# Retention and a SwiGLU layer on one core: units of 512 tokens, and an output product of 49 block products

## The chip, the cores and the metric

The kernel runs on one core of one Trainium2 chip. A core has TensorE (PE in the profile; its weight loads are listed apart as PEld), VectorE (DVE), ScalarE (ACT), GpSimd (POOL) and SyncE (SP), which issues most transfers. They work on an on-chip memory of 128 partitions (SBUF); TensorE writes its products to PSUM, eight banks of 512 float32 a partition. The metric is the time of one execution on the device, in microseconds.

## The reference

Retention over 8 batches of 8 heads (sequence 576, head size 64), then an RMS norm and a gated feed-forward layer on the 4608 tokens of 512 features. All matrix data is float32 but for the three weight matrices of the layer, which the kernel receives as float64 words and rounds itself.

```python
scores = scale * q @ k.T                      # per batch and head, 576 x 576
D[i, j] = gamma_h ** (i - j) if i >= j else 0 # gamma_h = 1 - 2**(-5 - h)
x = (scores * D) @ v                          # -> (4608, 512)
xn = x / sqrt(mean(x * x) + 1e-6) * rms_g
g, val = xn @ w_gate, xn @ w_val              # 512 -> 1536, twice
out = (g * sigmoid(g) * val) @ w_out          # 1536 -> 512
```

## The kernel before

A job is a pair of heads of one batch; `slot(j)` does the scores of job j in chunks of 64 rows, with a running state (`sums`), and finishes job j - 1. The feed-forward part runs in 12 units of U = 384 tokens. Units 0 and 1 multiply plainly while the weights are being rounded and combined. From unit 2 on, all products use a scheme that replaces 8 products of 2x2 blocks with 7, at the price of sums and differences of blocks: `up` for the two input products, `across` for the output product.

```python
U = 384; HU = U // 2; NH = 6                 # tokens of a unit, of a half, blocks of 128 of half of 1536
w_out = const.tile([P, NF, DM], F32)          # later four slots for blocks of w_out read back from DRAM
w_up = [const.tile([P, 7 * 2, NH * P], F32) for n in ("w_gate", "w_val")]   # all 7 blocks, resident

def up(u, m, g):                              # 3 g x 2 m of them per unit
    def product(blk, ps, start):
        for i in range(2):
            for c in range(2):
                nc.tensor.matmul(ps[:, i * HU : i * HU + HU], lhsT=w_up[m][:, 2 * blk + c, cut],   # L611
                                 rhs=t_of[u][blk][:, c], ...)
    # ... seven products, each followed by adds of the kind of add/result on VectorE (L618, L628):
    product(A22, w, False)
    result(f + NH, 0, "c21", u2, w)

def differences(u):                           # two block differences of h, 1152 elements each (L726)
    for o, a, b in ((t1, b12, b11), (b12, b22, b12)):
        nc.vector.tensor_tensor(out=o, in0=a, in1=b, op=ALU.subtract)

def across(u):                                # seven products of 12 matmuls, weights stationary
    def product(rhs, ps, start, ...):
        for i in range(2):
            for c in range(NH):
                nc.tensor.matmul(ps[:, i * HU : i * HU + HU], lhsT=a[:, c, i * P : i * P + P],     # L742
                                 rhs=rhs[:, c], ...)
    # ... x, z, w, y, x, z, w; block updates of h between them (L755), results turned by a
    #     32x32 transpose on VectorE (L764) and stored in rows of 32 elements

def root_1(u):                                # the norm of the next unit: mean of squares by a product
    nc.tensor.matmul(s, lhsT=ones, rhs=y, start=True, stop=True)                                   # L529
    # ... then two root steps on ScalarE and VectorE
# main loop, unit u: six up stages with up to four slots between them; then
rest = across(u); next(rest)                  # differences
behind(u, 5)                                  # a slot, then norm_0(u + 1): squares and three sums
for i, _ in enumerate(rest):                  # one step per product
    if i == 2: behind(u, 6)                   # root_1(u + 1)
    elif i == 3: root_2(u + 1)
    elif i == 4: behind(u, 7)                 # norm_2(u + 1): scaling of x, its differences
```

The rounding of the weights (`exponent`, `mantissa`, `join`) runs on VectorE and ScalarE during the first two units; GpSimd combines the blocks of w_gate and w_val (`combine`, L949) after that.

Of the kernel before, what the change touches and what calls it, by code (L numbers as in the profile page):

```python
# [14 lines left out]
P = 128  # L15
L = P // 2
# [25 lines left out]
def kernel(  # L42
# [21 lines left out]
    U = 384  # L64
# [3 lines left out]
    NH = NF // 2  # L68
    NG = NH // 2
    EPS = 1e-6  # L70
    K0, K1 = 2.38924456, 0.703952253
    assert (D, DM, NHP * P) == (64, H * D, DM) and S % SQ == 0 and NTOK % U == 0
    assert NC * L == S and NC == 2 * NFULL + 1 and TAIL == L == D and NHP == 4 and NH % 2 == 0
    assert (2 * S) % U == 0 and B % 2 == 0 and S == 3 * HU

# [4 lines left out]
    ffn = ctx.enter_context(tc.tile_pool(name="ffn", bufs=1))  # L80
    tmp = ctx.enter_context(tc.tile_pool(name="tmp", bufs=6))
    outs = ctx.enter_context(tc.tile_pool(name="outs", bufs=3))
# [22 lines left out]
    top = cell("top", 255.0 * 2.0**23)  # L105
    causal = const.tile([P, L], F32, name="causal")
# [8 lines left out]
    guess = cell("guess", 0x5F1FFFF9 + 2.0**22 * np.log2(DM))  # L115
    w_out = const.tile([P, NF, DM], F32, name="w_out")
# [3 lines left out]

    A11, A12, S1, A22, S2, S3, S4 = range(7)
    A21 = S1

    w_up = [const.tile([P, 7 * 2, NH * P], F32, name=n) for n in ("w_gate", "w_val")]

    CUT = HU // L
    parts = [(0, 0, NC), (1, 0, CUT), (1, CUT, NC)] + [(b, 0, NC) for b in range(2, B)]
    jobs = [(b, hp, c0, c1) for b, c0, c1 in parts for hp in range(NHP)]
    LATER_JOBS = 3 * NHP
    st = [{} for _ in jobs]
    x_of, t_of, h_of, first_places = {}, {}, {}, {}

    def tiles_of(j):

        return jobs[j][2] // 2, min((jobs[j][3] + 1) // 2, NFULL)

    def load_qk(j):
        b, hp, c0, _ = jobs[j]
        for nm, src in (("q", q), ("k", k)):

            t = raw.tile([P, S // SQ, SQ], F32, tag=nm + "raw", name=f"{nm}raw_{j}")  # L150
            for e in range(2):
                rows = src[b, 2 * hp + e, c0 * L :]
                rows = rows.rearrange("(t b) (i a) -> i b t a", b=SQ, a=SQ)
                for i in range(D // SQ):
                    r = e * D + i * SQ
                    nc.sync.dma_start(out=t[r : r + SQ, c0 * L // SQ :], in_=rows[i])
            st[j][nm + "raw"] = t

    def load_first(j, tails):

        b, hp, *_ = jobs[j]
        d = st[j]
        tiles = tiles_of(j)[1]
        room = h_of[0].rearrange("p f t -> p (f t)")
        part = room[:, j * 4 * P : j * 4 * P + tiles * P]
        d["q"] = part.rearrange("p (e t d) -> p e t d", e=2, d=D)
        nc.sync.dma_start(
            out=part.rearrange("p (e t) -> p e t", e=2),  # L170
            in_=q[b, 2 * hp : 2 * hp + 2, : tiles * P].rearrange("e (p t) d -> p e (t d)", p=P),
        )
        for nm, src in (("k", k), ("v", v)):
            t = first_places[nm][j][:, : tiles * P].rearrange("p (c e d) -> p c e d", e=2, d=D)
            d[nm] = t
            for e in range(2):
                nc.sync.dma_start(
                    out=t[:, :, e],
                    in_=src[b, 2 * hp + e, : tiles * P].rearrange("(c p) d -> p c d", p=P),
                )  # L180
            for n in (0, 1) if nm == "k" else (2,):
                load_tails(b, n, tails)

    def find_places():

        n = NFULL * 2 * D
        kv = {
            nm: [raw.tile([P, n], F32, tag=nm, name=f"first_{nm}_{i}", bufs=bufs) for i in range(bufs)]
            for nm, bufs in (("k", 4), ("v", 3))
        }  # L190
        other = raw.tile([P, S], F32, tag="qraw", name="first_k_7")[:, :n]
        sums = [ffn.tile([P, 3 * 2 * HU], F32, tag=t, name=f"first_{t}") for t in ("sums", "t1")]
        room = h_of[0].rearrange("p f t -> p (f t)")[:, 2 * NHP * 4 * P :]
        more = w_up[1][:, 8:].rearrange("p b f -> p (b f)")[:, 6 * DM :]
        return {
            "k": kv["k"] + kv["v"] + [other],
            "v": [t[:, i * n : i * n + n] for t in sums for i in range(2)]
            + [more[:, i * n : i * n + n] for i in range(3)] + [room],
        }

    def load_tails(b, n, heads):


        if heads:
            room = w_up[1][:, 8:].rearrange("p b f -> p (b f)")
            nm, src = (("qt", q), ("kt", k), ("vt", v))[n]
            t = room[:TAIL, (3 * b + n) * DM : (3 * b + n + 1) * DM]
            t = t.rearrange("p (h d) -> p h d", d=D)
# [7 lines left out]
    def load_kv(j):  # L216

        b, hp, *_ = jobs[j]
        i0, _ = tiles_of(j)
        for nm, src, bufs in (("k", k, 4), ("v", v, 3)):  # L220
            t = raw.tile([P, NFULL, 2, D], F32, tag=nm, name=f"{nm}_{j}", bufs=bufs)
            for e in range(2):
                rows = src[b, 2 * hp + e, i0 * P : NFULL * P]
                nc.sync.dma_start(
                    out=t[:, i0:, e], in_=rows.rearrange("(c p) d -> p c d", p=P)
                )
# [18 lines left out]
    def turn(j, waits=(0, 0)):  # L245


        d = st[j]
        n = tiles_of(j)[1]
        for nm in "qk":  # L250
            if nm == "k":
                warm_up(waits[0], 4 * P)
# [15 lines left out]
        if jobs[j][3] < NC:  # L268
            return
# [923 lines left out]
```

## Time and profile before

The time is 1136.91 us, the median of two runs (1136.47 and 1137.35); the profiled execution spans 1134.0 us.

| what | value |
|---|---|
| TensorE busy | 1118.2 us, 99% |
| VectorE, ScalarE, GpSimd busy | 732.3, 258.9, 39.5 us |
| moved | 126.73 MB, mean 112 GB/s |
| granted clock of TensorE, mean | 0.997 |
| window 0 to 45 us | TensorE busy 37.24 us, VectorE 30.98, 219 GB/s |
| window 242 to 331 us (unit 2) | TensorE busy 88.46 us of 89, VectorE 62.44, 120 GB/s |

How to read it: the busy table gives each engine's busy time and number of instructions; matmuls are pipelined, so a busy TensorE says only that products are in flight. The line of 40 digits gives the busy share by slice of 28 us. A group's line has the line number, engine, operation, output and inputs, their shape, the count, then the busy time of the group and the mean ns of one, then the idle time before it and what ended it. A timeline line has the start in us, how long the run of equal instructions took, the engine and the instruction. The chain of work that ended last is listed in order of time as start, duration, engine, tile and count.

### The profile page before, as it was taken

The numbers are of one execution on the slowest core, as the hardware profiler recorded it, in microseconds if no ns is written. First come the engines' busy times: TensorE is split into PE (matmuls) and PEld (weight loads), VectorE is DVE, ScalarE is ACT, GpSimd is POOL, SyncE is SP. The second block draws the span as 40 slices with busy tenths as digits, with TensorE's granted clock in tenths as the row PEclk, the third lists the DMA queues.
The fourth block names the chain that finished last, engine by engine and source line by source line (L and its number), as shares of the span: only waits on it lengthen the run. The fifth ranks groups of instructions, "written<-read, shape, count | busy, mean of one in ns | idle before, by whom it ended". The sixth has DMA issues, their size and how long they took to land.

```text
span 1134.0 us, 24783 instructions
## 1 busy us (share of the span) xinstructions
PE 1118.2 (99%) x10456; PEld 1042.7 (92%) x10456; DVE 732.3 (65%) x1452; ACT 258.9 (23%) x508; POOL 39.5 (3%) x68
## 2 busy tenths in 40 slices
PE   8899999999999999999999999999999999999998
PEld 6655567999999999999999999999999999999998
DVE  5888878556775784485677585465676666446352
ACT  5565551011212211211211121121120210120110
POOL 0100000560000000000000000000000000000000
PEclk9899999999999999999999999999999999999999
DMA  9743587336264474062552555215436503303304
GB/s 226 221 149 112 141 179 223 57 64 166 55 143 107 103 165 134 1 131 79 123 127 45 139 147 100 112 54 102 137 69 135 154 6 99 126 1 101 123 1 112
DMA packets 307040, 126.73 MB, mean 112 GB/s; under 512 B 284528, under 2 KB 289904, under 8 KB 306928
## 3 DMA queue, kind: packets, MB, share of 16 engines
q1 hardware_dynamic: 302640, 123.66, 43.1%
q8 instruction: 82, 1.34, 0.5%
q10 hardware_dynamic: 4288, 1.48, 0.5%
q14 instruction: 30, 0.25, 0.1%
HBM read 110.14 MB, written 14.94 MB: 110 GB/s over the span
## 4 chain that ended last, share of the span: by engine, by line
PE 93%; DVE 2%; DMA 2%; ACT 2%; issue 1%; SPq 0%; POOL 0%; POOLq 0%; DVEq 0%; ACTq 0%
PE x L611 14%; PE w L611 14%; PE z L611 14%; PE xo L742 8%; PE wo L742 8%; PE zo L742 8%; PE up L668 8%; PE y L611 7%; PE yo L742 4%; PE av L406 2%; PE s L323 1%; PE av L428 1%; PE s L345 1%; ACT w_gate L906 1%; PE ms L529 1%
## 5 line engine op out<-in xcount | busy, mean ns | idle before, releaser
L635 ACT COPY m<-x 128x384 f32<-128x384 f32 x60 | 28.8, 479 | 338.7 <-PE x L611 338.7
L742 PE MATMUL xo<-h,w_out 128*128 128x192 f32 x528 | 90.3, 328 | 0.0
L611 PE MATMUL x<-x,w_gate 128*128 128x192 f32 x480 | 88.8, 328 | 0.5 <-issue 0.5
L611 PE MATMUL w<-sums,w_val 128*128 128x192 f32 x480 | 88.6, 328 | 0.3
L611 PE MATMUL x<-x,w_val 128*128 128x192 f32 x480 | 88.7, 328 | 0.0
L611 PE MATMUL w<-sums,w_gate 128*128 128x192 f32 x480 | 87.9, 326 | 0.0
L611 PE MATMUL z<-x,w_gate 128*128 128x192 f32 x480 | 87.8, 326 | 0.0
L611 PE MATMUL z<-x,w_val 128*128 128x192 f32 x480 | 87.8, 326 | 0.0
L742 PEld LDWEIGHTS xo<-h,w_out 128*128 128x128 f32 x528 | 85.9, 190 | 0.6
L742 PE MATMUL wo<-h,w_out 128*128 128x192 f32 x504 | 85.6, 326 | 0.4 <-DVE c_last L790 0.4
L618 DVE TENSOR_TENSOR u<-m,y 128x384 f32<-128x384 f32 x60 | 33.1, 552 | 79.1 <-PE y L611 79.1
L742 PEld LDWEIGHTS wo<-h,w_out 128*128 128x128 f32 x504 | 82.4, 190 | 0.7 <-DVE c_last L790 0.7
L611 PEld LDWEIGHTS w<-sums,w_val 128*128 128x128 f32 x480 | 79.2, 190 | 2.7 <-DVE c L618 2.7
L611 PEld LDWEIGHTS x<-x,w_gate 128*128 128x128 f32 x480 | 79.2, 190 | 1.3 <-issue 0.8
L611 PEld LDWEIGHTS x<-x,w_val 128*128 128x128 f32 x480 | 79.1, 190 | 0.6
L611 PEld LDWEIGHTS z<-x,w_val 128*128 128x128 f32 x480 | 79.6, 190 | 0.0
L611 PEld LDWEIGHTS z<-x,w_gate 128*128 128x128 f32 x480 | 79.6, 190 | 0.0
L611 PEld LDWEIGHTS w<-sums,w_gate 128*128 128x128 f32 x480 | 79.5, 190 | 0.1
L618 DVE TENSOR_TENSOR h<-u,w 128x384 f32<-128x384 f32 x60 | 33.0, 550 | 69.8 <-PE w L611 69.8
L630 ACT ACTIVATE h<-h 128x384 f32<-128x384 f32 x90 | 47.0, 523 | 88.6 <-DVE h L618 88.6
L668 PE MATMUL up<-x,w_gate 128*128 128x384 f32 x192 | 63.8, 489 | 0.7 <-DVE x L580 0.7
L668 PE MATMUL up<-x,w_val 128*128 128x384 f32 x192 | 63.5, 488 | 0.2 <-DVE h L674 0.2
(189 smaller groups left out, 1779.5 us busy)
## 6 DMA issues: line engine op xcount, KB each, us to landing
w_out<-w_blocks SPq DMA_DIRECT2D x70, 768.0 KB, 4.9
out_dram<-o SPq DMA_DIRECT2D x364, 24.0 KB, 1.6
qraw<-in_q_dram SPq DMA_DIRECT2D x96, 72.0 KB, 2.7
kraw<-in_k_dram SPq DMA_DIRECT2D x96, 72.0 KB, 2.7
k<-in_k_dram SPq DMA_DIRECT2D x48, 128.0 KB, 2.8
v<-in_v_dram SPq DMA_DIRECT2D x48, 128.0 KB, 2.9
w_out<-in_moe_w_gate_dram SPq DMA_DIRECT2D x5, 1024.0 KB, 8.3
w_out<-in_moe_w_val_dram SPq DMA_DIRECT2D x3, 1024.0 KB, 5.2
```

Of the source, the lines that this page charges most:

```text
L323: nc.tensor.matmul(s[side(odd), e, i * L : i * L + L], lhsT=d["kT"][side(e), c * L : c * L + L], rhs=d["qT"][side(e), c * L : c * L + L], ...
L345: nc.tensor.matmul(o[side(e)], lhsT=d["k"][side(odd), i, e], rhs=d["v"][side(odd), i, e], start=True, stop=True,)
L406: mm = nc.tensor.matmul(av[odd][column(j, odd, e), i * L : i * L + L], lhsT=d["v"][side(odd), i, e] if c < NC - 1 else d["vt"][:, e], rhs= ...
L428: mm = nc.tensor.matmul(av[odd][column(j, odd, e), i * L : i * L + L], lhsT=d["sum"][c - 1][side(e)], rhs=d["qT"][side(e), c * L : c * L + L],
L529: nc.tensor.matmul(s, lhsT=ones, rhs=y, start=True, stop=True)
L611: nc.tensor.matmul(ps[:, i * HU : i * HU + HU], lhsT=w_up[m][:, 2 * blk + c, cut], rhs=t_of[u][blk][:, c], start=(start and i == c == 0), ...
L618: nc.vector.tensor_tensor(out=o, in0=a, in1=pairs_of(ps), op=ALU.add)
L630: nc.scalar.activation(out=o, in_=c, func=AF.Silu)
L635: nc.scalar.copy(out=s1, in_=pairs_of(x_))
L668: nc.tensor.matmul(ps[:, :U], lhsT=w_up[m][:, 4 * half + c, i * P : i * P + P], rhs=x_of[u][:, c], start=(c == 0), stop=(c == NHP - 1),)
L742: nc.tensor.matmul(ps[:, i * HU : i * HU + HU], lhsT=a[:, c, i * P : i * P + P], rhs=rhs[:, c], start=(start and i == c == 0), stop=False, ...
L906: nc.scalar.activation(func=AF.Relu, **acts.pop(0)[1])
```

## The change

Units become 512 tokens, 9 instead of 12. The output product splits each of its seven block products once more into seven (49 products of 128 tokens x 384 rows x 128 features), with the tokens' `h` blocks stationary and the weights moving, so that its result comes out with tokens on partitions and is stored in rows of 128 elements without a transpose. The inner sums of `h` run on GpSimd, as do the final block sums of a unit and the joining and combining of the weights. All weight blocks, of w_gate and w_val as well as w_out, are written to DRAM once and stream back from unit 2 on through one ring in SBUF. Batch 1 is no longer split into two sets of jobs, so there are 32 jobs instead of 36.

```diff
-    U = 384
+    U = 512
+    NK = NH // 2
...
-    w_out = const.tile([P, NF, DM], F32, name="w_out")
-    w_up = [const.tile([P, 7 * 2, NH * P], F32, name=n) for n in ("w_gate", "w_val")]
+    RING = 17920
+    ring = const.tile([P, RING], F32, name="ring")
...
+    UP, OUT = 7 * 2 * 2 * P, 7 * NK * P       # 1.84 and 1.38 MB over 128 partitions
+    def refill(most=len(pieces)):             # called whenever a piece has been used
+            nc.sync.dma_start(out=ring[:, a:z], in_=src)
...
     def across(u):
+        def inner_sums(n):                    # 128x384 each
+            for o, a, b, op in (
+                (i1, x12, x11, ALU.subtract), (i3, x22, x12, ALU.subtract),
+                (i2, i3, x11, ALU.add), (i4, x21, i2, ALU.subtract),
+            ):
+                nc.gpsimd.tensor_tensor(out=o, in0=a, in1=b, op=op)
+        def product(n, nm, w, late):
+            for s, lhs in (
+                ((S1, i1), (S3, i3), (S2, i2), (A22, i4)) if late
+                else ((A11, x[:, :NK, :P]), (A12, x[:, NK:, :P]), (S4, x[:, NK:, P:]))
+            ):
+                ps = vector[nm][s // 4][:, s % 4 * P : s % 4 * P + P]
+                for c in range(NK):
+                    nc.tensor.matmul(ps, lhsT=lhs[:, c], rhs=w[:, s, c], ...)      # L702
...
+        inner_sums(0)
+        inner_sums(1)
+        yield
+        for n, nm in enumerate("xzwyxzw"):    # x, y, z, w: two PSUM banks each, eight in all
+            product(n, nm, w, False)
+            yield
+            product(n, nm, w, True)
+            ...                               # block updates of h and t1, 1536 elements each, on VectorE;
+            ...                               # adds of PSUM to the sums of the unit (896 elements)
+            if n + 2 < 7:
+                inner_sums(n + 2)
+            yield
+        if not last:
+            combine()                         # seven sums of 128x4x128 on GpSimd; on VectorE in the last unit
...
     for u in range(2, NU):
...
             rest = across(u)
+            if u + 1 < NU:
+                norm_0(u + 1)
             for i, _ in enumerate(rest):
-                if i == 2:
-                    behind(u, 6)
+                if i == 0:
+                    root_1(u + 1)
+                elif i == 4:
+                    root_2(u + 1)
+                elif i == 8:
+                    norm_2(u + 1)
...
+    def join(i):                              # half a chunk of weights: 512 elements
+        nc.gpsimd.tensor_tensor(out=o, in0=x, in1=e, op=ALU.mult)
+    def combine_blocks(t, o21):               # four sums of 512; for w_out four more of 7x128
+            nc.gpsimd.tensor_tensor(out=t[o], in0=t[x], in1=t[y], op=op)
...
+        for u, k in (                         # plain up stages of units 0 and 1, four steps each
+            (0, 0), (0, 1), (1, 0), (1, 1), (0, 2), (1, 2), (0, 3), (1, 3), (0, 4), (0, 5), (1, 4),
+            (1, 5),
+        ):
+            weights_to(READY[k])              # READY = (4, 8, 12, 20, 28, 32) of 36 halves
```

The two sets of w_gate and w_val that lie in SBUF at a time in the plain stage are reused: the halves of set k + 2 are joined only after both units have used set k. In the plain stage `across(0)` and `across(1)` follow each other directly.

## The prediction

> **What bounds the kernel now.** I read the page's busy table and its 40 slices first, then the chain that ended last in order of time, then the groups by shape, and last the timeline and the single-line views around the operations that the change adds.
>
> ```profile
> PE 1118.2 (99%) x10456; PEld 1042.7 (92%) x10456; DVE 732.3 (65%) x1452; ACT 258.9 (23%) x508; POOL 39.5 (3%) x68
> PE   8899999999999999999999999999999999999998
> DVE  5888878556775784485677585465676666446352
> PE 93%; DVE 2%; DMA 2%; ACT 2%; issue 1%; SPq 0%; POOL 0%; POOLq 0%; DVEq 0%; ACTq 0%
> ```
>
> TensorE is busy in every slice and is 93% of the chain; only the first 2 slices have slack. GpSimd does nothing after slice 9. So time can be won only by giving TensorE fewer or cheaper instructions, and lost by making it wait. Its price list comes from the chain (start, us, instructions):
>
> ```profile
> 61.84 67.35 PE up L668 x208
> 404.25 3.90 PE zo L742 x24
> ```
>
> A float32 product is two instructions, each with its own weight load. 67.35/208 = 324 ns for 384 moving columns and 3.90/24 = 162.5 ns for 192: 0.84 ns a column and about 1 ns more. By that, 256 columns cost 216 ns, 512 cost 431, 128 cost 109. Loads are hidden at 192 columns. At 128 columns a load of 128 columns may not be; the only place with loads closer together is the mean of squares, whose moving operand has one column (TensorE, then its loads):
>
> ```profile
> 39.86 0.83 PE L515 MATMUL ms<-mean_w,sq 128*128 128x1 f32 x6 [1.00 <-DVE sq L503]
> 39.86 0.74 PEld L515 LDWEIGHTS ms<-mean_w,sq 128*128 128x128 f32 x6 [1.24 <-DVE sq L503]
> ```
>
> Six loads take 0.74 us with the last one's 0.19 us to its end: (0.74 - 0.19)/5 = 110 ns from load to load. So 128 x 128 x 128 should run at about 111 ns an instruction, set as much by the load as by the product.
>
> GpSimd's price for a tensor_tensor, from the view of one line (min/median/max ns), and one VectorE operation beside it:
>
> ```profile
> L949 POOL TENSOR_TENSOR w_val<-w_val x12: 1267/1272/2262, 211.6 to 227.2; 128x512 f32<-128x512 f32 x12
> L949 POOL TENSOR_TENSOR w_gate<-w_gate x12: 1265/1273/2262, 228.4 to 244.0; 128x512 f32<-128x512 f32 x12
> L755 DVE TENSOR_TENSOR h<-h x22: 1315/1350/1755, 219.0 to 1121.7; 128x1152 f32<-128x1152 f32 x22
> ```
>
> 1.27 us for 512 elements, 1.35 us from one to the next (16.2 us for 12 in the groups). The two outliers of 2262 ns are a wait of 0.99 us each. One of them covers 219 us, where L755, with both inputs in SBUF, took 1755 ns instead of 1350: each waited for the other. VectorE operations with one input in PSUM, which ran beside GpSimd in the same stretch, kept their usual time.
>
> Last, the end of an up stage today:
>
> ```profile
> 396.30 1.57 PE L611 MATMUL w<-sums,w_val 128*128 128x192 f32 x8
> 397.91 0.55 DVE L618 TENSOR_TENSOR c<-u,w 128x384 f32<-128x384 f32 x1
> 400.08 4.17 PE L742 MATMUL xo<-h,w_out 128*128 128x192 f32 x24
> 407.91 0.56 DVE L499 SCALAR_TENSOR_TENSOR sq<-sq,sq 128x384 f32<-128x384 f32 x1
> 411.88 0.81 PE L529 MATMUL ms<-sq,ones 128*128 128x384 f32 x2
> ```
>
> The last square sum (L499) is ready at 408.5, 10 us after the last up product, but the product that needs it (L529) stands behind three output products and doesn't wait.
>
> **What the Trainium skill says.** "TensorE: Matmul & The Clock Gate", section "LDWEIGHTS (loading the stationary operand)": the load's time follows its columns over 1.2 GHz, an estimate of 107 ns for 128; the trace's 110 agrees. "GPSIMD Engine Reference", section "3.1 Elementwise — side-by-side cycle accounting": about 2.6 cycles an element for two inputs, an estimate of 1.1 us for 512 at the 1.2 GHz of its table of specifications; the trace has 1.27. "Advanced Engine Details and Errata", section "GPSIMD Details": GpSimd shares a read and a write interface with VectorE and conflicts with VectorE instructions with two SBUF inputs; the 2262 and 1755 ns agree. The first page's section on the HAM clock gate says that an idle stretch of some 3.4 us halves TensorE's clock; the trace before has no such gap after its start, so nothing here shows it.
>
> **The change, part by part: TensorE's own work.** Before: output 12 units x 168 x 162.5 ns = 328 us; up 10 x 336 x 162.5 = 546; plain up 2 x 192 x 324 = 124; together 998. After: output 9 units x 49 blocks x 3 x 2 = 294 instructions x 111 ns = 32.6 us each, 294 together; up 7 x 336 x 216 ns = 72.6 each, 508; plain up 2 x 192 x 431 = 166; together 968. **30 us are won**, all of it in the output product; up and plain up together neither gain nor lose.
>
> Rest of TensorE's path, without new waits. The first feed-forward product starts at 48 us before; five full attention slots instead of eight (four of them short) stand ahead of it, but the whole norm of unit 0 follows them unhidden: 45 us. Between feed-forward products the timeline before shows 2.35 us for a later attention job; 20 of these are 47 us. Three early and four late jobs in the plain stage with their turns: 20 us. Seven norm products of 512 columns: 6 us. Tail (seven block sums on VectorE, stores): 4 us. 968 + 45 + 47 + 20 + 6 + 4 = **1090 us**, if nothing new waits.
>
> **New waits.** (a) *The norm product at the head of the output stage.* The changed program puts the 512-column product of L464, for the next unit, straight after the last up product and ahead of the first output product, because the output stage needs all eight banks afterwards. It needs the sum of four squares, and in VectorE's order that stands behind c21 (add, multiply), two differences and three gathers. VectorE takes 0.55 us for 384 elements and 1.35 for 1152, so about 0.69 for 512: 0.25 + 7 x 0.72 = 5.3 us after the last up product. All but the first have two SBUF inputs, and GpSimd is at its h sums then; each turn it takes costs one of its operations, 1.0 us (512 to 384 elements by the ratio, 0.95, and the gap): with two or three turns 7 to 8 us. TensorE stands for that time in units 2 to 7: 6 x 7 = **42 us**.
>
> (b) *The sums of unit 0 ahead of the h sums of unit 1.* They are seven GpSimd operations of 512 elements, 9.4 us, and come only after the last add of unit 0 (1.4 us); then four h sums, 4.2 us. The late half of unit 1's first product could start after 2 us and starts after 15: **13 us**, once.
>
> (c) *GpSimd's pace in the output stage.* Four h sums are 4.2 us for each product of 42 x 111 ns = 4.7 us: it keeps up, with 0.5 us to spare. But two-input work of VectorE in the same stage is two block updates of 1536 (1.75 each), three gathers, three root operations and eight of the norm (0.69 each), 13 us a unit. If all of it pushed GpSimd back, the six rounds of h sums after the first would need 25 + 13 = 38 us against 30 until the last is needed. Part of it falls into (a) and into GpSimd's idle time; I take 2 to 3 us for each of six units: **15 us**.
>
> (d) *The plain stage.* GpSimd now joins 36 half chunks (1.35 each), combines six sets (5.4 each) and three slices of w_out (about 14.6 each, the 7x128 sums at 2.3): 125 us. 103 of them lie between step 12 and the end of the stage, a stretch of some 130 us; between steps 12 and 24 it is 36 of 41 us, and VectorE's two-input mantissa work (two of 0.64 us a half) pushes against it. Without the conflict it fits; with all of it, 12 halves x 1.3 us = 16 us make the stage late by 10, and later sets by as much again. I take **15 us**.
>
> Sum: 1090 + 42 + 13 + 15 + 15 = **1175 us**.
>
> **Rivals.** *The gain arrives.* If GpSimd and VectorE hardly meet and (a) is as short as VectorE's own 5.3 us, (a) 32 and (b) 13 remain: 1135, within 2%. For a time under 1114 the wait of (a) must not exist; the program's order speaks against that. *GpSimd becomes the bound.* If the conflict is a strict taking of turns, (c) is 6 to 8 us a unit, 45, (d) is 40, and (a) 50: 1238. The two outliers of 0.99 us speak for turns; but they are two, and most of GpSimd's 24 operations met no such VectorE work. *Transfers bind.* A main unit now moves 11 MB of up and 9.6 MB of output blocks besides 4 to 5 MB of attention: 25 MB in some 120 us, 210 GB/s, against 118 to 120 before; in the output stage 1.38 MB each 4.7 us, 290 GB/s. The first slices reached 226 GB/s with small packets, and the ring holds some five pieces ahead; I expect no wait from this, but should it be one, 3 us a piece over 63 pieces would be far over 1240. *The load isn't hidden* beside a product of its own length: if load and product don't overlap fully at 128 columns and an instruction takes 130 ns, the output stage costs 9 x 294 x 19 ns = 50 us more, though GpSimd's lateness would hide some of it.
>
> **Range and chances.** 1175 us; 1125 (only (a) at its shortest and (b), with a somewhat lower base) to 1225 (turns taken nearly strictly). Under 1114: 0.08. Within 2% (1114 to 1160): 0.27. Slower by over 2%: 0.65.
>
> **What would show it.** Output instructions at 111 ns inside a run of 18 or 24; a gap of 5 to 9 us on TensorE ahead of each L464 product of units 3 to 8, released by the VectorE gather (L429); one of about 13 us early in unit 1's output stage, released by GpSimd (L688); GpSimd operations of 384 elements near 1.0 us with outliers of 1.5 to 2; late halves of some output products released by GpSimd. I'd be wrong if the gap at L464 is under 3 us, if output instructions take over 120 ns, or if releases by DMA of the ring head the list of TensorE's waits.

## The result, and the profile after

The changed kernel takes **1336.5 us** (median of 1335.33 and 1337.71) against 1136.9 before: a ratio of 1.175, with a 95% interval of 1.172 to 1.179. The prediction said slower, but 1175 us in a range that ended at 1225. 161 us more than predicted are to be explained.

The page of the changed kernel: first TensorE's busy time, then three of its lines of 40 slices (33 us each) with the granted clock, then the chain's shares.

```profile
PE 1140.5 (85%) x10086; PEld 937.8 (70%) x10086; DVE 790.6 (59%) x1328; ACT 297.5 (22%) x581; POOL 507.3 (38%) x400
PE   6488967377476999799979997998899799979997
POOL 0312363555167810470066007401730272056026
PEclk7788988689688999899989998999899999989999
DVE 1%; issue 0%; DVEq 0%
```

Before, TensorE had 9s from the third slice on. Now there are two kinds of holes: the first 13 slices are ragged throughout, and from then on one slice in four is a 7 or 8, once for each unit. In both the granted clock (PEclk, in tenths of full speed) dips below 9; before, it did so in the second slice alone. The chain reaches back only 7 us here, to the last sums, so it can't tell where the rest went; the list of TensorE's waits can (total us, times, longest):

```profile
PE up L637 <- POOL ring L871: 51.4, 8, 17.4
PE ms L464 <- DVE sq L429: 42.6, 6, 7.1
PE s L280 <- DVE kT L252: 18.0, 3, 17.6
...
PE ms L445 <- DVE sq L433: 12.5, 1, 12.5
PE s_out L702 <- POOL vi L688: 11.6, 1, 11.6
```

L637 is the plain up product of units 0 and 1, and L871 the join of a half chunk of weights. The second and fifth lines are the waits that steps (a) and (b) named; the first is step (d)'s, over three times as long as I took all of (d) to be.

The end of an up stage, the same place as the last view of before:

```profile
548.44 0.69 DVE L585 TENSOR_TENSOR c<-u,w 128x512 f32<-128x512 f32 x1 [0.31 <-PE w L578]
...
551.10 2.88 DVE L433 TENSOR_TENSOR sq<-sq,sq 128x512 f32<-128x512 f32 x2
...
554.09 1.29 DVE L429 SCALAR_TENSOR_TENSOR sq<-sq,sq 128x512 f32<-128x512 f32 x1
...
555.52 2.04 PE L464 MATMUL ms<-sq,ones 128*128 128x512 f32 x2 [7.12 <-DVE sq L429]
...
557.36 2.64 PE L702 MATMUL s_out<-ring,h 128*128 128x128 f32 x18
```

TensorE has nothing from 548.4 to 555.5. Three gathers take 4.2 us because GpSimd is at its h sums; three in the plain stage, with GpSimd at none, took 0.69 each, 2.1. After the wait two instructions of L464 take 2.04 us and the 18 of L702 2.64 (1.10 and 2.17 in e6 below, without the wait): the record of the clock is at half from 551.5 to 558.3, so L464 and the first of L702 run at half clock. Further into the stage an output instruction comes every 111.5 ns, as worked out.

GpSimd's h sums (min/median/max ns), answering the GpSimd lines of before:

```profile
L688 POOL TENSOR_TENSOR vi<-h x80: 992/998/2595, 339.5 to 1317.1; 128x384 f32<-128x384 f32 x80
L688 POOL TENSOR_TENSOR vi<-t x36: 997/1449/2516, 371.2 to 1321.2; 128x384 f32<-128x384 f32 x36
```

1.0 us undisturbed, with a median of 1.45 for the sums of `t`, which at this place fall beside VectorE's products, differences and gathers.

Now the plain stage, which holds most of the loss. Lines of the timeline from four engines, in order of time (SPq is SyncE's queue: when a transfer was issued):

```profile
176.20 15.57 POOL L880 TENSOR_TENSOR vi<-vi 128x512 f32<-128x512 f32 x8
185.32 2.37 DVE L857 SCALAR_TENSOR_TENSOR ring<-ring 128x512 f32<-128x512 uint32 x1
191.80 8.47 SPq L891 DMA_DIRECT2D w_out_blocks<-vi  x7
193.07 8.83 PE L637 MATMUL up<-x,ring 128*128 128x512 f32 x16 [12.09 <-POOL ring L871]
200.37 1.48 SPq L821 DMA_DIRECT2D sums<-in_moe_w_val_dram  x1
207.04 0.43 DVE L834 TENSOR_SCALAR sums<-sums 128x512 uint32<-128x512 uint32 x1 [19.35 <-DMA sums<-in_moe_w_val_dram]
210.88 2.08 PE L637 MATMUL up<-x,ring 128*128 128x512 f32 x2 [8.97 <-POOL ring L871]
```

Read it downward. GpSimd makes the eight block sums of a w_out slice for 15.6 us; the join that TensorE needs stands behind them in its order (12.09 us). The seven stores of that slice can't go before 191.8 and take 8.5 us to issue, and the load of the next half chunk stands behind them in SyncE's order, until 200.4. VectorE, which would round it, has nothing for 19.35 us, and TensorE stands again (8.97). No engine is busy throughout: in the 296 us from 72 to 368 TensorE is busy 216, VectorE 165, ScalarE 109, GpSimd 118.

### The profile page after: what moved, and what is told of

The parts are those of the page before. It is cut to its first block, busy times and chain, and to the rows that moved or that the text cites. A ratio compares the mean times of both kernels' runs of the same rounds, so it can differ in the third digit from the quotient of the medians.

```text
span 1335.9 us, 24285 instructions
## 1 busy us (share of the span) xinstructions
PE 1140.5 (85%) x10086; PEld 937.8 (70%) x10086; DVE 790.6 (59%) x1328; ACT 297.5 (22%) x581; POOL 507.3 (38%) x400
## 5 line engine op out<-in xcount | busy, mean ns | idle before, releaser
L688 POOL TENSOR_TENSOR vi<-h 128x384 f32<-128x384 f32 x80 | 95.6, 1213 | 512.6 <-DVE h L595 460.6
L637 PE MATMUL up<-x,ring 128*128 128x512 f32 x384 | 186.3, 643 | 56.0 <-POOL ring L871 51.4
L637 PEld LDWEIGHTS up<-x,ring 128*128 128x128 f32 x384 | 76.9, 206 | 159.9 <-issue 88.8
L578 PE MATMUL x<-x,ring 128*128 128x256 f32 x672 | 161.4, 383 | 0.0
L578 PE MATMUL z<-x,ring 128*128 128x256 f32 x672 | 158.8, 379 | 0.0
L578 PE MATMUL w<-sums,ring 128*128 128x256 f32 x672 | 158.7, 379 | 0.0
L578 PEld LDWEIGHTS z<-x,ring 128*128 128x128 f32 x672 | 127.7, 190 | 17.4
L578 PEld LDWEIGHTS w<-sums,ring 128*128 128x128 f32 x672 | 127.7, 190 | 17.4
L578 PEld LDWEIGHTS x<-x,ring 128*128 128x128 f32 x672 | 125.1, 190 | 17.4
L578 PE MATMUL y<-sums,ring 128*128 128x256 f32 x336 | 79.4, 379 | 2.2 <-DVE sum L329 2.2
L702 PE MATMUL s_out<-ring,vi 128*128 128x128 f32 x540 | 69.0, 282 | 11.6 <-POOL vi L688 11.6
L702 PEld LDWEIGHTS s_out<-ring,vi 128*128 128x128 f32 x540 | 65.7, 198 | 12.1 <-POOL vi L688 12.0
L702 PEld LDWEIGHTS s_out<-ring,h 128*128 128x128 f32 x384 | 54.7, 224 | 22.0 <-DVE vi L720 8.3
L702 PE MATMUL s_out<-ring,h 128*128 128x128 f32 x384 | 56.4, 309 | 13.3 <-DVE vi L720 6.8
```

The source lines that it names most:

```text
L578: nc.tensor.matmul(ps[:, i * HU : i * HU + HU], lhsT=w[:, blk, c, i * P : i * P + P], rhs=t_of[u][blk][:, c], start=(start and i == c == 0 ...
L637: nc.tensor.matmul(ps, lhsT=w[:, blk, c % 2, i * P : i * P + P], rhs=x_of[u][:, c], start=(c == 0), stop=(c == NHP - 1),)
L688: nc.gpsimd.tensor_tensor(out=o, in0=a, in1=b, op=op)
L702: nc.tensor.matmul(ps, lhsT=lhs[:, c], rhs=w[:, s, c], start=((nm, s // 4) not in first), stop=False, skip_group_check=True,)
```

## Experiments

Each changes the changed kernel unless it says otherwise. "Stage" is the time from the first plain up product to the first output product, "units 2 to 8" from the first product of `up` to the last product (trace). The times of e10 to e12 are medians of four executions, the others of e1 to e14 are single ones; executions of one kernel side by side differed by up to 4.2 us. The kernel before took 1134.4 to 1138.9 us beside them.

For the plain stage I had three theories. A: SyncE's order, stores that wait ahead of loads and fetches. B: GpSimd and VectorE hinder each other, so that their work takes longer than its sum. C, formed after e1 to e4: pieces are made just in time, and rounding stands still where a join may not go yet. For units 2 to 8 the theory was step (a), the late norm product, and its rival GpSimd's pace.

| run | time, us | first up product at | stage | units 2 to 8 |
|---|---|---|---|---|
| changed kernel | 1336.5 | 71.8 | 303.2 | 866.8 |
| e1_stores_held | 1301.4 | 72.1 | 262.9 | 872.3 |
| e2_norm_later | 1303.8 | 72.1 | 302.0 | 834.2 |
| e3_all_held | 1312.9 | 69.5 | 282.9 | 866.2 |
| e4_joins_on_vector | 1309.1 | 70.6 | 271.1 | 873.1 |
| e5_rounds_ahead | 1305.9 | 71.9 | 270.8 | 867.4 |
| e6_norm_early | 1289.3 | 73.2 | 302.1 | 819.2 |
| e7_start | 1335.8 | 65.9 | 312.9 | 863.0 |
| e8_kept_busy | 1325.4 | 72.2 | 302.3 | 855.6 |
| e9_stores_gpsimd | 1312.5 | 72.1 | 278.9 | 866.8 |
| e10_combined | 1261.6 | 68.2 | 278.8 | 818.6 |
| e11_sets_first | 1249.7 | 68.1 | 269.6 | 817.5 |
| e12_sums_on_vector | 1242.1 | 65.9 | 259.0 | 818.9 |
| e13_no_rounding (leaves out work) | 1224.0 | 51.9 | 210.3 | 867.4 |
| e14_no_block_sums (leaves out work) | 1273.5 | 69.1 | 241.8 | 867.4 |

**e1: stores held back.** The stores of finished blocks are issued three half chunks later, behind the loads.

```diff
-            nc.sync.dma_start(out=w_out_d[o][:, :, k], in_=slices[:, o])
+            held.append((n_joined, lambda o=o: nc.sync.dma_start(...)))   # the same for w_up_d
...
             load_half(i + 4, nc.sync)
+            send(i - 3)
```

> The changed kernel, but the stores of finished weight blocks (L885, L891) are issued three half chunks later, so that the loads of the next halves and of q and k no longer stand behind them in SyncE's order. Theory A (SyncE's order: stores that wait for GpSimd's sums hold up the next loads): the three waits of VectorE for a load in the plain stage (19.4, 16.6, 17.3 us) go, and about 45 us of the 1336.5 with some of TensorE's half-clock time: 1280 to 1295. Theory B (GpSimd and VectorE hinder each other at the shared interface): the loads were no limit, under 15 us: 1322 to 1335.

1301.4, between the two ranges. The waits of up products for joins fell from 51.4 to 25.6 us and the one of 17.6 us for kT went: SyncE's order was a cause. But the last slice's stores now stood behind the attention's fetches, and the first output product waited 19.1 us for its blocks: part of the gain was handed back at the next door.

**e2: norm product later.** In units 2 to 7 `root_1` stands behind the first output product instead of ahead of it.

```diff
-                if i == 0:
+                if i == 2:
                     root_1(u + 1)
```

> The changed kernel, but the norm product of the next unit stands after the first output product instead of ahead of it. If the product waits for VectorE alone, the six gaps of 7.5 us and the half-clock time after each go: 6 x (7.5 + 1 to 2) = 50 to 57 us, 1280 to 1287. If GpSimd sets the pace of the output stage (part (c) of the prediction), the time comes back there as waits for h sums: 1300 to 1336.

1303.8, all of it in units 2 to 8. The number is in the rival's range, but not for its reason: no new wait for h sums is in the list. The wait for the gathers fell from 7.1 to 2.4 us a unit (the gap that I had counted, which holds the norm product too, from 9.3 to 4.3 to 4.6): they are still late for the new place. Five of these six short waits are followed by a record of 3.4 us at half clock, so it doesn't take 7 us of idleness.

**e3: block sums held too.** The sums and stores of a finished block stand four half chunks later.

```diff
-            (finish_set if kind == "up" else finish_slice)(k)
+            held.append((i, lambda: finish(k)))                           # sent four halves later
```

> The changed kernel, but both the block sums on GpSimd and their stores are issued four half chunks later, after the joins of the next set. Theory A and GpSimd's order together: TensorE's waits for joins (51 us for L871, 18 us for kT) nearly go, with the half clock after them: 1255 to 1275, 15 to 30 us under the run that holds the stores alone. If only SyncE's order counts: the same as that run. Theory B: 1322 to 1335, the conflicts being the same.

1312.9, in none of the three ranges and worse than e1, with waits for joins of 36.8 us, the longest 19.1, and 18.7 us again ahead of the first output product. A later place in the order moved the 15 us of a slice's sums ahead of another join.

**e4: joins and block sums on VectorE.**

```diff
-        nc.gpsimd.tensor_tensor(out=o, in0=x, in1=e, op=ALU.mult)         # join
+        nc.vector.tensor_tensor(out=o, in0=x, in1=e, op=ALU.mult)
-            nc.gpsimd.tensor_tensor(out=t[o], in0=t[x], in1=t[y], op=op)  # combine_blocks
+            nc.vector.tensor_tensor(out=t[o], in0=t[x], in1=t[y], op=op)
```

> The changed kernel, but joins and block sums of the weights run on VectorE instead of GpSimd, in the same order. Theory B: the two engines no longer meet in the plain stage, VectorE's weight operations fall back to 0.43 and 0.69 us, which saves some 42 us there against 63 us of added work, and the waits for GpSimd go: 1270 to 1300. Theory A: the stores still stand ahead of the loads, waiting now for VectorE: the loads stay late, 1320 to 1360.

1309.1, above B's range and below A's. What GpSimd had cost VectorE is in the groups. The changed kernel, 72 to 370 us (busy us, mean ns):

```profile
L850 DVE SCALAR_TENSOR_TENSOR ring<-ring 128x512 uint32<-128x512 uint32 x15 | 22.5, 1501 | 1.1 <-ACT ring L828 0.9
L853 DVE TENSOR_SCALAR ring<-ring 128x512 uint32<-128x512 uint32 x15 | 15.8, 1050 | 0.5
```

The same groups of e4, 72 to 335 us, and the slices' sums there:

```profile
L880 DVE TENSOR_TENSOR vi<-vi 128x512 f32<-128x512 f32 (+1 forms) x24 | 21.4, 891 | 0.7
L850 DVE SCALAR_TENSOR_TENSOR ring<-ring 128x512 uint32<-128x512 uint32 x15 | 10.3, 685 | 0.2 <-ACT ring L828 0.2
L853 DVE TENSOR_SCALAR ring<-ring 128x512 uint32<-128x512 uint32 x15 | 6.4, 430 | 0.5
```

L850 falls from 1501 to 685 ns and L853 from 1050 to 430; a slice's sum takes 0.89 us where GpSimd took 1.81 on average (1.42 for 512 elements, 2.20 for 896). So GpSimd did slow VectorE, by 2.2 and 2.4 times in these groups. Those of the halves in `t` were not slowed (684 and 430 ns), those in `sums` only in L850 (996). GpSimd itself lost little: without rounding beside them (e13) its sums took 1.27 and 2.08. VectorE now did 34.7 us of block sums and the stage was still 32 us shorter, but TensorE waited 18.0 us for joins, now VectorE's, and 9.4 for ScalarE's steps of the rounding.

**e5: rounding ahead.** e1's held stores (now four half chunks later, the last slice's soon after its last join), and exponent and mantissa work go on, up to four halves ahead, while a join waits for its place in the ring.

```diff
-            while not free_for(*halves[i][:2]):
-                yield
+            # joins when free_for allows, else exponent/mantissa of the next halves
```

> The stores of finished weight blocks are issued four half chunks later, as in the run with held stores, but the last slice's go out a step after its last join; and the exponent and mantissa work of the next halves goes on (up to four halves ahead) while a join has to wait for its place in the ring. Theory C (just-in-time order: rounding stands still until a set's place is free, and then TensorE waits for it): of the 303 us of the plain stage 80 to 95 go, the waits of up products for GpSimd's ring writes fall from 51 us to under 15, and the time is 1240 to 1265. Theory B (VectorE and GpSimd hinder each other, their work is what takes the time): moving work earlier changes nothing beyond what held stores gave: 1285 to 1310.

1305.9, theory B's number, not C's. Waits for joins fell to 13.0 us, but those of attention for kT rose to 22.2; ahead of the longest, 10.7 us, the fetches stood behind the stores of the last slice (issued from 298.2 to 307.2). With one queue for everything, an order that spares one of its users makes another wait.

**e6: norm early.** Squares and gathers of the next unit stand beside the last up stage, in the part of `vi` that the h sums use only later.

```diff
+                    if u + 1 < NU and n == NHP + 1 and 1 <= i <= NHP:
+                        square_early(u + 1, i - 1)      # square and gather of one quarter
...
-            if u + 1 < NU:
-                norm_0(u + 1)
+            if u + 1 < NU:
+                root_1(u + 1)
```

> Squares and gathers of the next unit in units 2 to 7 stand beside the last up stage instead of behind it, in SBUF that the h sums don't use yet; the norm product is then ready when TensorE comes to it. If the 9.3 us gap ahead of it and the half clock that follows it are one cause, both go: 6 x 9.3 = 56 us and 6 x 3 to 4 = 21 us, 1255 to 1270, and a unit's period falls from 128 to 115 to 117 us. Rival (GpSimd's pace in the output stage is next in line, as the four h sums of a product take 4.2 of its 4.7 us and start no earlier): late halves wait for GpSimd, half of the gain is lost, 1290 to 1305.

1289.3, just below the rival's range, and 47.6 us less in units 2 to 8: **step (a) is this**. TensorE's timeline of e6 at the end of the same up stage:

```profile
548.00 1.10 PE L470 MATMUL ms<-vi,ones 128*128 128x512 f32 x2 [0.17 <-DVE vi L429]
548.93 2.17 PE L710 MATMUL s_out<-ring,h 128*128 128x128 f32 x18
550.94 2.84 PE L710 MATMUL s_out<-ring,vi 128*128 128x128 f32 x24
```

The wait is 0.17 us instead of 7.12, and the instructions behind it run at full clock. The rival (GpSimd's pace is next in line) isn't seen: late halves waited 3 us in all. I had expected 77 us; I had counted the gap of 9.3, which holds the product itself, as if all of it could go.

**e7: the start.** Last gather and norm of unit 0 ahead of four halves of mantissa work; the small write `tick` on GpSimd.

```diff
             one(j)
+            if j == NHP:
+                gather(*squares.pop())
+                norm_1(0)
...
-        d["valued"] = nc.scalar.copy(out=tick, in_=mhalf[:1])
+        d["valued"] = nc.gpsimd.memset(tick, 0.0)
```

> The last gather and the norm of unit 0 stand ahead of four half chunks of mantissa work on VectorE, and the small write that separates two products on the same banks is GpSimd's again instead of ScalarE's. If these two waits make the start long, the first feed-forward product comes at 55 to 60 us instead of 71.75 and the time falls to 1320 to 1325. Rival (VectorE's whole work before that point sets the start, whatever its order): the first product comes at 68 to 72 and the time stays at 1330 to 1337.

The first up product came 5.8 us earlier (expected: 12 to 17), and the time didn't change: on GpSimd the `tick` stood behind a slice's sums, and attention waited up to 17.5 us for a write of one number.

**e8: kept busy.** Eight products of 512 columns, whose results are thrown away, ahead of each norm product of units 3 to 8.

```diff
+        if u > 2:
+            for _ in range(8):
+                nc.tensor.matmul(s, lhsT=ones, rhs=x_of[u][:, 0], start=True, stop=True)
         nc.tensor.matmul(s, lhsT=ones, rhs=y, start=True, stop=True)
```

> Eight products of 512 columns whose results are thrown away stand ahead of each norm product of units 3 to 8, so that TensorE is busy for 6.9 us while it would wait 7.1. The wait stays, only the idleness goes. If idleness brings the half clock, the output instructions after it run at 111 ns from the first, the half-clock records at 551, 678, 807, 937, 1067 and 1183 us go, and 6 x 3 to 4 = 18 to 24 us are saved: 1312 to 1320. Rival (the half clock has another cause): the time stays at 1333 to 1340 and the records stay.

1325.4: the wait is filled, nothing else is changed, and 11.2 us go, 1.9 a unit. TensorE at the same place in e8:

```profile
547.55 7.03 PE L466 MATMUL ms<-x,ones 128*128 128x512 f32 x16
554.76 1.13 PE L467 MATMUL ms<-sq,ones 128*128 128x512 f32 x2 [0.18 <-DVE sq L429]
555.72 2.17 PE L705 MATMUL s_out<-ring,h 128*128 128x128 f32 x18
```

The 18 instructions behind the norm product take 2.17 us as in e6, and the half clock record at 551 is gone. So the idle 7 us bring the half clock, and of e6's 47.6 us some 11 were that; I had put it at 18 to 24. It is the half clock after an idle stretch that the prediction cites. The length of one gap alone doesn't settle it, though: e2's 2.4 us were mostly followed by it too, and in the trace before, the record of half clock from 41.0 to 47.9 us follows a gap of 1.0.

**e9: stores on GpSimd's queue.** GpSimd issues the stores after its own sums, so that SyncE never waits for them.

```diff
-            nc.sync.dma_start(out=w_out_d[o][:, :, k], in_=slices[:, o])
+            nc.gpsimd.dma_start(out=w_out_d[o][:, :, k], in_=slices[:, o])   # and w_up_d
```

> One change: the stores of finished weight blocks are issued by GpSimd, which makes the last sums they wait for, instead of SyncE. The order of everything else stays. Theory A (SyncE takes its transfers in order, and a store that waits for GpSimd holds the loads of the next half chunks and the attention's fetches behind it): all that holding the stores back won in the plain stage (60 us) comes, and the wait of 19 us ahead of the first output product that it brought doesn't, nor the 17.6 us wait for kT: 1265 to 1290. Rival (the work of the two engines is what takes the time, or issuing costs GpSimd as much as it saves): 1305 to 1335.

1312.5, the rival's range. The 17.6 us wait for kT went and the first output product no longer waited for blocks, but waits for joins stayed at 45.3 us, the longest 23.2: issuing seven stores keeps GpSimd from the next join for 5.2 us more (188.9 to 194.1).

**e10: all orders mended.** e9, e5's rounding ahead, e6, the norm of the start as in e7 with `tick` back on ScalarE, and unit 0's final sums behind unit 1's first h sums (`combine()` moved from the end of `across(0)` to the first step of `across(1)`).

> All orders mended at once, no work taken away: stores on GpSimd's queue, rounding up to four halves ahead of a join that waits, squares and gathers of the next unit beside the last up stage, the block sums of unit 0 behind the first h sums of unit 1, and the norm of unit 0 ahead of the last mantissa work of the start. If the waits found are independent, the parts measured or seen alone add up: 1336 less 47 (norm early), 35 to 60 (stores), 12 (sums of unit 0), 6 (start) and 0 to 20 (rounding ahead): 1190 to 1235. If the order was nearly all of the excess over my working, the plain stage falls to some 215 us and the time to 1150 to 1190. Rival (GpSimd's and VectorE's work in the plain stage is the bound once the waits on transfers are gone): the plain stage stays over 250 us, with waits for GpSimd's ring writes at their head, and the time at 1235 to 1260.

1261.6, just above the rival's range; the ratio to before is 1.110 (1.108 to 1.112). The 11.6 us of step (b) are gone (for 6.2 at the norm product beside it) and units 2 to 8 are as in e6, but the stage is still 278.8 us: the rival's case. GpSimd's timeline of e10 and TensorE's line beside it:

```profile
163.70 15.51 POOL L890 TENSOR_TENSOR vi<-vi 128x512 f32<-128x512 f32 x8
179.50 6.53 POOL L901 DMA_DIRECT2D w_out_blocks<-vi  x7 [0.29 <-POOL vi L890]
184.72 3.88 POOL L881 TENSOR_TENSOR ring<-ring 128x512 f32<-128x512 f32 x2
187.40 11.18 PE L647 MATMUL up<-x,ring 128*128 128x512 f32 x20 [7.79 <-POOL ring L881]
```

21 us in one piece, from 163.7 to 184.7, stand ahead of the joins of set 3: 15.5 of sums, then 5.2 of issuing (the 6.53 of the line overlap the first join).

**e11: sets first.** e10 with another order of the pieces.

```diff
-        ("up", 0), ("up", 1), ("up", 2), ("out", 0), ("up", 3), ("out", 1), ("up", 4), ("up", 5), ("out", 2)
+        ("up", 0), ("up", 1), ("up", 2), ("up", 3), ("out", 0), ("up", 4), ("out", 1), ("up", 5), ("out", 2)
-    READY = (4, 8, 12, 20, 28, 32)
+    READY = (4, 8, 12, 16, 24, 32)
```

> As the combined kernel, but the order of the rounded pieces is changed: set 3 comes before the first slice of w_out and the second slice behind set 4, so that no set stands behind the eight sums (15.5 us) and seven stores (6.5 us) of a slice in GpSimd's order just before TensorE needs it. In the combined kernel TensorE waited 8 us at 179 and 20 us at 223 for such a set, with a half clock behind each. If GpSimd's order is what is left of the plain stage's excess, these two waits and their half clocks go and the plain stage falls from 274 to 235 to 245 us: 1220 to 1232. If the amount of GpSimd's work is the bound, the waits come back at sets 4 and 5 and the time stays at 1250 to 1265.

1249.7 (ratio 1.099, 1.096 to 1.102), between the two: of four waits for joins one is left, but it is 17.0 us long (at 237), and up to 6.9 us are now waited for VectorE's evictions.

**e12: sums on VectorE.** e11 with e4's two lines; GpSimd only issues stores.

> The kernel with sets first, and the joins and block sums of the weights on VectorE instead of GpSimd, whose queue then only issues the stores. In the kernel with sets first TensorE waited 17 us at 237 and 7 us at 196 while GpSimd was at a slice (15.6 us of sums at 1.95 each, twice VectorE's pace, and 6.5 us of issuing), and VectorE's own steps took 1.4 to 2.4 us instead of 0.43 to 0.69 beside it. If the choice of engine (GpSimd's slower operations and the pushing) is what keeps the plain stage at 264 us, VectorE does a slice's sums in 7 us without being pushed, and the stage falls to 215 to 235: 1200 to 1222. If VectorE then becomes the bound (its 163 us of busy time in the stage, less some 40 of inflation, plus 36 joins of 0.69 and 48 sums of 0.69 to 1.1, about 180 of 264) its order delays the evictions, TensorE's waits move to VectorE, and the time stays at 1235 to 1255.

1242.1 (ratio 1.094, 1.091 to 1.096), the best of the runs that do all the work, but in neither range: nearer the second. TensorE's up products now wait mostly for VectorE's evictions (L653) and only once for a join (L881):

```profile
PE up L647 <- DVE h L653: 14.0, 5, 6.0
PE up L647 <- DVE ring L653: 7.1, 1, 7.1
PE up L647 <- DVE ring L881: 3.8, 1, 3.8
```

VectorE, and then TensorE, at the longest of them:

```profile
220.84 7.37 DVE L890 TENSOR_TENSOR vi<-vi 128x512 f32<-128x512 f32 x8
228.46 0.68 DVE L653 TENSOR_TENSOR ring<-ring,up 128x512 f32<-128x512 f32 x1
229.20 6.56 PE L647 MATMUL up<-x,ring 128*128 128x512 f32 x8 [7.13 <-DVE ring L653]
```

The eviction stands behind a slice's eight sums in one piece, as the joins did on GpSimd. On either engine, in the two splits tried, TensorE meets the weights' work.

**e13 and e14: what the weights cost by themselves.** e13 leaves out the loading and rounding of the weights: a half of a block is filled with a constant by GpSimd where it would be joined. Block sums, stores and products stay. e14 leaves out the block sums: the blocks that they would write hold a constant. Loads, rounding, joins, stores and products stay.

```diff
-        nc.gpsimd.tensor_tensor(out=o, in0=x, in1=e, op=ALU.mult)         # e13: and load_half,
+        nc.gpsimd.memset(o, 0.01)                                         # exponent, mantissa empty
-        combine_blocks(...)                                               # e14: three calls
+        nc.gpsimd.memset(...)                                             # once for each buffer
```

> The changed kernel without the loading and the rounding of the weights: a half of a block is filled with a constant by GpSimd where it would be joined; block sums, stores and all products stay. What the plain stage costs when nothing has to come from VectorE, ScalarE and the weight loads. If the rounding chain (load, exponent, ScalarE, mantissa, join, one half after another) is what makes the stage 303 instead of my 201 us, it falls to 200 to 220, and the start by 5 to 10 us: 1225 to 1245. If GpSimd's block sums and the stores behind them are enough to hold TensorE up, the waits of up products for GpSimd's ring writes remain (over 30 us of 51) and the stage stays over 245: 1270 to 1290.

> The changed kernel without the block sums of the weights: the blocks that they would write hold a constant, written once by GpSimd; loads, rounding, joins, stores and all products stay. If the sums on GpSimd (21 us for a slice, with what they push VectorE back and keep the stores and the loads behind them waiting) are the larger part of the excess, the plain stage falls from 303 to 225 to 240 us: 1258 to 1275. If the rounding chain alone is enough to hold TensorE up, the stage stays at 265 to 290: 1300 to 1325.

e13: 1224.0 us, just under the first range, a stage of 210.3 us, and the first product at 51.9, 20 us sooner where I had expected 5 to 10. e14: 1273.5, in the first range, a stage of 241.8 and the first product at 69.1. The stage in e13, from 52 to 254 us (length; busy us of TensorE, its loads, VectorE, ScalarE and GpSimd, each with its count; then the granted clock, the share of the DMA engines and GB/s):

```profile
52.00:254.00 202.00, 196.70 (x1486) 96.47 (x1486) 61.71 (x158) 30.05 (x72) 80.86 (x75) 0.98 0.46 125
```

and in the changed kernel from 72 to 368:

```profile
72.00:368.00 296.00, 215.62 (x1486) 102.98 (x1486) 165.49 (x281) 109.27 (x194) 117.69 (x80) 0.85 0.49 136
```

The same 1486 TensorE instructions take 202 us at 0.98 of the clock when no weights are loaded and rounded, and 296 at 0.85 when they are. Of the 94 us between, 75 are idle (80.4 against 5.3 us without a product in flight), and 19 are the same products taking longer (215.6 against 196.7), at half clock. In e13 GpSimd still does all its block sums (busy 81 us, constants included), and no up product waits for one; in e14 the rounding is all there, and of the 51.4 us of waits for joins this is left:

```profile
PE up L637 <- POOL ring L878: 10.4, 5, 3.5
```

So of the 93 us that the weights' preparation costs (303.2 - 210.3), 61 need the rounding chain **and** the block sums in its way: they go without either. The other 32 stay without the sums (241.8 - 210.3): they are the chain's own, with its joins and the stores.

## Why the prediction was wrong

Where the 161 us are, by its own terms (trace):

| term | taken | measured | excess |
|---|---|---|---|
| start to the first up product | 45 | 71.8 | 27 |
| plain stage: products 165.5, attention 20, **step (d) 15** | 200.5 | 303.2 | 103 |
| output of units 0 and 1, with (b) 13 | 79 | 87.2 | 8 |
| units 2 to 8, with (a) 42 and (c) 15 | 845 | 866.8 | 22 |
| tail | 4 | 7 | 3 |

They add up to 163 (the rounded terms taken give 1173.5), against 161 between prediction and median. Sorted by cause, an estimate from e13, e6, e10 and the list of waits: 78 are step (d), 20 the rounding in the start, and some 75 the 1090 us that I had taken for TensorE's path without new waits (7 at the start, 25 in the plain stage, 10 in the output of units 0 and 1, 31 in units 2 to 8, 3 at the end); (a) is 6 over its term, (b) and (c) 16 under theirs.

- **TensorE's own work: right in the price of an instruction, low in the rest of the path.** Output instructions come at 111.5 ns, so the rival of the load that isn't hidden (130 ns) is out. But units 2 to 8 in e6, without the wait of (a), take 825 us to the end for 3584 tokens, 230 ns each; before, units 2 to 11 took 892 us for 3840, 232 ns. By the prices the products save 7.8 ns a token, 28 us; 7 are left. In e6 the steps from one output instruction to the next are 118.5 ns on average, 14 us over the 111.5 (waits of 1.2 us at most, for VectorE's adds above all), and the 20 attention jobs take 56 us instead of 47.
- **(a) right, size low.** 42 taken; 42.6 of waiting by the list of waits and 11.2 of half clock (e8), which I had left out; e6 won 47.6 of the two together.
- **(b) right.** 13 taken; 11.6 of waiting, gone when the sums moved (e10).
- **(c) wrong, and little.** 15 taken; GpSimd keeps pace: in units 2 to 8 the list has no wait of an output product for it, and those for VectorE's adds (L720) are 0.9 us at most, 5.9 together.
- **(d) failed, and it is the miss.** I took "15 us" for the plain stage. The 303.2 are 210.3 without the weights' preparation (e13) and 93 for it, six times the 15. The 210.3 were 185.5 in my sum: attention, norm and the first blocks' transfer are 25 more than the 20 I took. The step added up GpSimd's busy time, 125 us in all, and asked whether 103 of them fit into some 130 us, and 36 into 41. As a sum that was no mistake: in e13 the block sums are all there in a stage of 210, and no up product waits for them. What it didn't ask is in which order the pieces stand. A half chunk goes load, VectorE, ScalarE, VectorE, GpSimd, and only then may the next load into its place go; there are four places, and every store and fetch is in the same SyncE queue. One slice's 15.6 us of sums in one piece stops the other engines in turn, and in the end GpSimd itself (idle for 15.2 us before its join at 209.5), and the half clock behind a stop is added. How much is order alone is shown in part: other orders, with the stores on GpSimd's queue, bring the stage to 269.6 (e11), 34 us, and the other engine for joins and sums 11 more (e12). Whether the remaining 49 of the 93 could go with the same work isn't shown. The skill's "DMA: Bandwidth & Descriptors", section "Anatomy of one DMA — SWDGE (gpsimd) path", says that a wait is held by the sequencer that issues and not by the DMA engine; the loads at 200.4 behind the stores at 191.8 show it, and I didn't use it.
- **The conflict in (d) was also undersized.** I counted VectorE's two-input steps, "two of 0.64 us a half". L853 has a single input and was pushed from 430 to 1050 ns just the same. "Advanced Engine Details and Errata", section "Mode Summary", tells that a fast mode with two read ports exists, whose instructions conflict with GpSimd as well; that a step of 430 ns runs in it is my inference from its rate (1.2 elements a ns against 0.75 in L850), not shown.
- **The start, 45 us, failed too.** e13 reaches the first up product at 51.9: 20 of the 27 us go with the loading and rounding of the first weights, whose steps share VectorE's queue with the norm of unit 0. Mending that order won 6 of them (e7), or 4 (e10).
- **Rivals.** "GpSimd becomes the bound" took (c) for the place and 40 us for (d): the wrong place and still too small. "Transfers bind" is not seen: the ring's blocks were late once, by 6.6 us. "The gain arrives" failed with (a), whose wait was 7.1 us a unit and not VectorE's own 5.3, and with (d).

What stays open: how far the plain stage could come down with the same work. e12's 259 us is the best that was tried; the 210 of e13 is what it takes without rounding. Even that, with e6's and (b)'s gains taken off (1224 - 48 - 12 = 1164, an estimate from e13, e6 and e10), would not reach the time before: the base of 1090 was too low for that.

## What to carry to other kernels

When work moves to an idle engine, don't ask whether its sum fits into the stage: follow one piece through all the queues it passes, and ask what else stands in each queue ahead of it, in the order of the program. A long block of work that nobody needs soon, and its stores, ahead of a short one that TensorE needs now, can cost most of its length on each engine in the chain (here 15.6 us of sums brought TensorE waits of 12.1 and 9.0), and a half clock after it. Take a suspected stage's work away once, part by part, before mending orders: two such runs (e13, e14) told more than the changes of order ahead of them.

## What the runs showed of the hardware

- VectorE steps on 512 elements in the plain stage (halves in `ring`), with GpSimd's sums beside many of them: 1501 ns on average against 685 with the sums moved (e4) for two inputs, 1050 against 430 for one; single ones up to 2.4 us.
- GpSimd's block sums of a slice: 1.27 us for 512 elements and 2.08 for 896 without VectorE's rounding (e13), 1.42 and 2.20 beside it; VectorE does them in 0.69 and 1.09 (e4).
- A store of a slice's block, issued by GpSimd, occupies it about 0.75 us: seven, and then the next join, from 179.5 to 184.7 (e10).
- A gap of 7.1 us on TensorE is followed by half clock that costs 1.9 us; products thrown away in the gap win those back (e8). Gaps of 2.4 us were followed by 3.4 us of half clock in five of six units (e2).
